# A second place for the residual sum, transposes that write every fourth column, and scales stored as 16 bytes per row

## The chip, the cores and the metric

The kernel runs on one core of a Trainium2 chip. The metric is the device time of one execution in microseconds (us). The kernel before took 1941.72 us, the median of 3 runs (1937.23 to 1942.7). The core has five engines with a queue each: TensorE (PE, with its weight loads listed apart as PEld), VectorE (DVE), ScalarE (ACT), GpSimd (POOL) and SyncE (SP, which here issues every DMA). An instruction that waits holds up all that stands behind it in its engine's queue.

## The reference

The input x is 8 images of 3136 positions by 256 channels. First stage: a real FFT over the positions, a complex 256x256 product with a bias, soft thresholding by 0.01, and the inverse FFT. Second stage, on its result x:

```python
X = np.fft.fft(x, axis=1); X = np.fft.fft(X, axis=2)
u = x + np.real(X)
un = (u - mean(u)) / sqrt(var(u) + 1e-6)      # per position, over 256 channels
out = u + relu(un @ w_ch1) @ w_ch2            # 256 -> 1024 -> 256
```

## The kernel before, in words

All transforms are matrix products. The 3136 positions are split as 64 x 49, so each image passes through a product over 64 (p1), one over 49 (p2_f2), the complex product with the weights (p2_w), the second FFT over channels (p2_mix), and back (p2_yt, p2_g2); these stages exchange their results through DRAM. Phase 3 then works on blocks of 128 positions. An even image has 24 blocks, in 6 groups of 4; an odd one has 25, in groups of 4, 4, 4, 4, 4, 2 and 3. That makes 52 groups for 8 images.

For each group phase 3 does this:

- p3_norm takes the last product of the inverse transform from PSUM and adds the term of the second FFT (line 714, tile ut, 128 positions x 256 channels, two blocks per tile, four buffers). It computes mean and variance, and from them rs, the reciprocal standard deviation of each position. The rs of a group are stored to a DRAM tile rd (line 737). The mean needs no correction later, as w1 and w2 are centred when they are loaded.
- p3_tr transposes ut on PE into PSUM (line 779, tile g_ut, one of the four "g" banks), so that channels lie on partitions, and splits it into a rounded half uth (ACT, line 781) and the remainder utl (DVE, line 156). Channels come as two halves k of 128. Before the change one step handles one pair of blocks with both halves k; a group of four blocks has two steps.
- p3_mlp1 multiplies by w1 (tile h) in eight slices f; each product is done as three products of halves. ReLU and the split into hh and hl follow (lines 798 and 799). After that POOL adds uth and utl into total (line 806), the residual, in four pieces of 256 columns. From then on uth and utl are free.
- p3_mlp2 multiplies by w2 into two PSUM banks (tile o) over the same eight slices. Between them it loads rb, the rs of the group spread over all partitions, from rd (line 824). At the end DVE multiplies o by rb (line 830; the second product is written into rb itself), adds it to total (line 833), and SP stores total to the output (line 834).

total has the tag "tot" with one buffer: the sum of a group can be written only when the stores of the group before have landed. The tile af, which holds the input of p2_f2 (line 446 loads it, two per quarter q of an image, lines 477 multiply), has three buffers of the same size, 4 KB per partition. cv_pair, a temporary of the weight split at the start, also lies in "tot".

Each stage is a generator that yields a due time; a heap runs them in order of these times, so that the instructions of many groups and images are interleaved in one program. Transposes are due from TR = -0.86 group times before their group, MLP 1 from 0 to 1, total at 1.0, and MLP 2 lags by MLAG/8 = 0.234. A planner of the framework then schedules the program by these priorities against its own model of time: an instruction moves forward to where the model finds its inputs and a free buffer. The order in each engine's queue is fixed at compile time; buffers are guarded by semaphores.

Of the kernel before, what the change touches and what calls it, by code (L numbers as in the profile page):

```python
# [10 lines left out]
F32 = mybir.dt.float32  # L11
F32R = mybir.dt.float32r
# [128 lines left out]
def spectral_block(ctx: ExitStack, tc: tile.TileContext, x, w_ri, b_ri, w1, w2,  # L141
# [30 lines left out]
    def split_double(name, h, l, parts, centred):  # L172

        def tmp(tag, bufs, dt=I32):
            return sb.tile([128, 512], dt, tag=tag, bufs=bufs, name=f"cv_{name}_{tag}")

        def v(t, sl):
            return t.rearrange("p (f e) -> p f e", f=h[sl].shape[1]) if len(h[sl].shape) == 3 else t  # L180

        both = []
        spare = centred and parts[0][0][2].start
        if spare:
            pair = sb.tile([128, 2, 512], F32R, tag="tot", bufs=1, name="cv_pair")
        for sl, raw in parts:
            hi, low = raw[:, 1::2], raw.bitcast(U16)[:, 1::4]
            tf = tmp("mt", 2, F32)
            sc.activation(tf, hi.bitcast(F32), AF.Abs, scale=65536.0)
            va.tensor_scalar(tf, tf, HI_MIN * 65536.0, HI_MAX * 65536.0, op0=ALU.max, op1=ALU.min)  # L190
            t = tf.bitcast(I32)
            va.tensor_scalar(t, t, 3, 0x7FFFFFFF, op0=ALU.logical_shift_left, op1=ALU.bitwise_and)
            w = tmp("ut", UTB)
            va.scalar_tensor_tensor(w, hi, -0x80000000, t, op0=ALU.bitwise_and, op1=ALU.bitwise_or)
            e = tmp("mt", 2)
            va.tensor_scalar(e, w, -0x800000, None, op0=ALU.bitwise_and)
            rf = pair[:, len(both)] if spare else tmp("ut", UTB, F32R)
            va.scalar_tensor_tensor(rf, low, 2.0 ** -36, e.bitcast(F32), op0=ALU.mult, op1=ALU.mult)
            both.append((sl, w.bitcast(F32), rf))
        if centred:  # L200
            mean = ps.tile([128, 512], F32, tag="h", bufs=2, name="mean")
            for i, (sl, wf, rf) in enumerate(both):
                te.matmul(mean, ones, wf, start=i == 0, stop=False)
                te.matmul(mean, share, rf, start=False, stop=i == 1)
            for sl, wf, rf in both:
                va.tensor_sub(wf, wf, mean)
        for sl, wf, rf in both:
            sc.copy(h[sl], v(wf, sl))
            va.tensor_sub(v(wf, sl), v(wf, sl), h[sl].bitcast(F32))
            va.tensor_add(l[sl], v(wf, sl), v(rf.bitcast(F32), sl))  # L210
# [230 lines left out]
    def rows_f2(b, q, s):  # L441

        u0 = 8 * q
        af = sb.tile([98, 4 * D], F32, tag="af", bufs=3, name="af")
        ad, u = a_dram[b](u0 + 4 * s)
        ld = nc.sync.dma_start(out=af.rearrange("p (u d) -> p u d", d=D), in_=ad.rearrange("n r c u d -> (n r c) u d")[:98, u:u + 4])
        tff = sb.tile([98, 4, 100], F32, tag="tff", bufs=3, name="tff")
        nc.sync.dma_start(out=tff, in_=c_tf[:, u0 + 4 * s:u0 + 4 * s + 4, :])
        if b == 0:
            af_ld[2 * q + s] = ld.ins  # L450
            done.add(("af", 2 * q + s))
        return af, tff
# [256 lines left out]
    def p3_norm(b):  # L709

        def finish(m, n, g, mt):

            ut = sb.tile([128, 2, D], F32, tag="ut", bufs=UTB, name="ut")
            va.tensor_add(ut[:, :n], g[:, :n * D].rearrange("p (n d) -> p n d", d=D), mt)
            gi, g0, z = [(i, g0, z) for i, (g0, z) in enumerate(GROUPS[b % 2]) if g0 <= m < g0 + z][0]
            if m == g0:
                scales[b, gi] = sb.tile([128, 4, 1], F32, tag="rs", bufs=4, name="rs")
            rall = scales[b, gi]
            rs = rall[:, m - g0:m - g0 + n]
            st = sb.tile([128, 2, 6], F32, tag="st", bufs=1, name="st")  # L720
            ag = sb.tile([128, 2, 2], F32, tag="ag", bufs=2, name="ag")
            for j in range(n):
                va.bn_stats(st[:, j], ut[:, j])
                va.bn_aggr(ag[:, j], st[:, j])
            vv = sb.tile([128, 2, 1], F32, tag="vv", bufs=1, name="vv")
            sc.activation(rs, ag[:, :n, 1:2], AF.Sqrt, bias=eps_t)
            gp.tensor_scalar(vv[:, :n], ag[:, :n, 1:2], 1.0, EPS, op0=ALU.mult, op1=ALU.add)
            va.reciprocal(rs, rs)

            gp.tensor_mul(vv[:, :n], vv[:, :n], rs)  # L730
            gp.tensor_mul(vv[:, :n], vv[:, :n], rs)
            gp.tensor_scalar(vv[:, :n], vv[:, :n], -0.5, 1.5, op0=ALU.mult, op1=ALU.add)
            gp.tensor_mul(rs, rs, vv[:, :n])
            uts[b, m] = ut
            if m + n == g0 + z:
                rd = scales[b, gi] = dr.tile([512], F32, tag="rd", bufs=4, name="rd")
                st_eng.dma_start(out=rd[:128 * z].rearrange("(j p) -> p j", j=z), in_=rall[:, :z].rearrange("p j o -> p (j o)"))
        for m, n in [(4 * i, 4) for i in range(6)] + [(NM - 1, 1)] * (b % 2):
            t0, T3 = clock3(b, m)
            yield t0 + T3 * (NRM - 0.5 * (n == 1))  # L740
            yield from after(("b", b), ("m", b))
            mt = sb.tile([128, 4, D], F32, tag="mt", bufs=2, name="mt")
            bfs = [sb.tile([128, 512], F32, tag="bf", bufs=4, name="bf") for _ in range(1 + (n > 1))]
            for r in range(2):
                if n == 1:
                    nc.sync.dma_start(out=bfs[0][64 * r:64 * r + 64, :D], in_=b_dram[b - 1 + r][m, 0].rearrange("c u d -> (c u) d"))
                else:
                    nc.sync.dma_start(out=bfs[r].rearrange("p (n d) -> p n d", d=D), in_=n2_rows(b_dram[b], m + 2 * r, 2))
            for r in (1, 0):
                bb, n2 = (b - 1 + r, m) if n == 1 else (b, NM * r + m)  # L750
                mpn, mmn = (d[0:NH].rearrange("(a n2) d -> a n2 d", n2=N2) for d in m_dram[bb])
                p = 64 * r
                nc.sync.dma_start(out=mt[p + 32:p + 64, :n][:, ::-1], in_=mmn[:, 49 - n2 - n:49 - n2])
                nc.sync.dma_start(out=mt[p:p + 32, :n], in_=mpn[:, n2:n2 + n])
            if n == 1:
                g = gtile("g_g1")
                te.matmul(g[:, :D], inv_f, bfs[0][:, :D], start=True, stop=True)
                finish(m, 1, g, mt[:, :1])
                continue
            banks = [gtile("g_g1") for _ in range(2)]  # L760
            quarters(banks, inv_f, [[bfs[r][64 * p:64 * p + 64] for r in range(2)] for p in range(2)], bfs[0][0:1, 0:2])
            for p, g in enumerate(banks):
                finish(m + 2 * p, 2, g, mt[:, 2 * p:2 * p + 2])

    def p3_tr(b):
        for gi, (g0, z) in enumerate(GROUPS[b % 2]):
            t0, T3 = clock3(b, g0)
            for i, n in parts_of[z]:
                yield t0 + T3 * (TR + i / 4)
                if i == 0:  # L770
                    uth = sb.tile([128, 2, 512], F32R, tag="uth", bufs=UTHB, name="uth")
                    utl = sb.tile([128, 2, 512], F32R, tag="utl", bufs=2, name="utl")
                    uthl[b, gi] = uth, utl
                ut = uts.pop((b, g0 + i))
                g = gtile("g_ut")
                gv = g.rearrange("p (k t) -> p k t", k=2)
                for j in range(n):
                    for k in range(2):
                        te.transpose(gv[:, k, j * 128:(j + 1) * 128], ut[:, j, k * 128:(k + 1) * 128], ident)  # L779
                tw = slice(i * 128, i * 128 + n * 128)  # L780
                sc.copy(uth[:, :, tw], gv[:, :, :n * 128])
                lo_v(utl[:, :, tw], gv[:, :, :n * 128], uth[:, :, tw])

    def p3_mlp1(b):
        for gi, (g0, z) in enumerate(GROUPS[b % 2]):
# [13 lines left out]
                va.scalar_tensor_tensor(hl[:, :w], h[:, :w], 0.0, hh[:, :w].bitcast(F32), op0=ALU.max, op1=ALU.subtract)  # L799
                hhl[b, gi, f] = hh, hl  # L800
            yield t0 + T3 * 1.0
            total = sb.tile([128, 2, 512], F32, tag="tot", bufs=1, name="total")
            for k in range(2):
                for c in range(0, w, D):
                    cols = slice(c, min(w, c + D))
# [3 lines left out]
    def p3_mlp2(b):  # L809
        for gi, (g0, z) in enumerate(GROUPS[b % 2]):  # L810
            t0, T3 = clock3(b, g0)
            w = z * 128
            for f in range(8):
# [5 lines left out]
                for k, o in enumerate(ops):  # L819
                    es = slice(k * 128, k * 128 + 128)  # L820
                    mm3(o, w2h[:, f, es], w2l[:, f, es], hh[:, :w], hl[:, :w], start=f == 0, stop=f == 7, first=1)
                if f == 1:
                    rb = sb.tile([128, 512], F32, tag="rb", bufs=1, name="rb")
                    nc.sync.dma_start(out=rb[:, :w], in_=scales.pop((b, gi))[:w].partition_broadcast(128))
            total = uthl.pop((b, gi))
# [105 lines left out]
```

## Time and profile before

| | |
|---|---|
| median of 3 runs | 1941.72 us |
| profiled execution, its own time | 1940.12 us |
| span of its instructions | 1938.3 us |
| mean granted TensorE clock | 0.973 |
| DMA queue of the program, share of 16 engines | 52.3% |

The profile is of a single execution. Its span runs from the first to the last instruction; 1.8 us lie around it. Busy shares are averages over the span. An idle time names what ended it, and a wait for several things is put down to the one that came last. In a timeline row the columns are start, duration, engine, line, operation, written tile <- read tiles, shape and count, and in brackets the idle time of the engine before it and who ended it.

### The profile page before, as it was taken

To read this page: it belongs to the slowest core of one execution; us is meant where nothing else is said; L and a number is where in the kernel's file an instruction comes from. 1 tells how busy PE (TensorE), PEld (TensorE's weight loads), DVE (VectorE), ACT (ScalarE), POOL (GpSimd) and SP (SyncE) were. 2 spreads that over 40 slices of the span, in tenths; PEclk is the share of its full clock that TensorE was granted. 3 is DMA by queue.
4 is the path that set the end of the run, shared out by engine and by line. 5 is a ranking of instruction groups with operands and counts; after the bars stand their busy time and mean duration, and the time that the engine had idled before them with its cause. 6 is when DMAs were issued, how large, how long until landed. Compare 5 with 4: busy or idle time off the path is not lost.

```text
span 1938.3 us, 29340 instructions
## 1 busy us (share of the span) xinstructions
PE 1841.4 (95%) x10044; PEld 1504.3 (78%) x10044; DVE 1192.2 (62%) x2603; ACT 807.5 (42%) x1864; POOL 560.4 (29%) x1028
## 2 busy tenths in 40 slices
PE   7886999899999999999999999999999999989998
PEld 4565787688787888877788788887878888867788
DVE  3664766566565766666666566656656656645543
ACT  2563544344444434444343444444444444322222
POOL 0003333222333422323323243332233433212121
PEclk8997999999999999999999999999999999999999
DMA  8763866455535756476444765546543543336211
GB/s 249 221 201 108 191 158 128 114 140 128 148 91 123 168 117 145 76 184 144 99 116 118 163 154 115 105 123 165 130 133 81 143 99 85 75 86 112 62 37 33
DMA packets 176365, 245.59 MB, mean 127 GB/s; under 512 B 42640, under 2 KB 123608, under 8 KB 175960
## 3 DMA queue, kind: packets, MB, share of 16 engines
q1 hardware_dynamic: 176216, 243.72, 52.3%
q8 instruction: 79, 1.29, 0.4%
q14 instruction: 70, 0.57, 0.1%
HBM read 140.79 MB, written 102.86 MB: 126 GB/s over the span
## 4 chain that ended last, share of the span: by engine, by line
PE 74%; DMA 12%; DVE 6%; POOL 3%; SPq 2%; issue 2%; ACT 2%; DVEq 0%; POOLq 0%; ACTq 0%
PE h L166 23%; PE o L166 23%; PE g_w L166 7%; PE g_f L477 4%; PE g_g L166 3%; DMA out_dram<-total 3%; PE g_g L377 2%; PE g_yt L665 2%; DMA mt<-md 2%; DMA bd<-bev 2%; PE g_ut L779 2%; PE g_f L377 2%; DMA xf<-in_x 2%; DMA md<-mq 1%; POOL total L806 1%
## 5 line engine op out<-in xcount | busy, mean ns | idle before, releaser
L799 DVE SCALAR_TENSOR_TENSOR hl<-h,hh 128x512 fp32r<-128x512 f32 (+2 forms) x416 | 273.1, 657 | 382.2 <-ACT hh L798 375.9
L798 ACT ACTIVATE hh<-h 128x512 fp32r<-128x512 f32 (+2 forms) x416 | 238.5, 574 | 417.3 <-PE h L166 396.5
L166 PE MATMUL o<-hl,w2h 128*128 128x512 f32 (+2 forms) x832 | 333.8, 401 | 9.9 <-DVE hl L799 7.6
L166 PE MATMUL h<-utl,w1h 128*128 128x512 f32 (+2 forms) x832 | 325.6, 391 | 2.8 <-DVE utl L156 2.8
L166 PE MATMUL h<-uth,w1l 128*128 128x512 f32 (+2 forms) x832 | 320.8, 386 | 0.0
L166 PE MATMUL h<-uth,w1h 128*128 128x512 f32 (+2 forms) x832 | 319.4, 384 | 0.0
L166 PE MATMUL o<-hh,w2l 128*128 128x512 f32 (+2 forms) x832 | 318.5, 383 | 0.0
L166 PE MATMUL o<-hh,w2h 128*128 128x512 f32 (+2 forms) x832 | 318.3, 383 | 0.0
L806 POOL TENSOR_TENSOR total<-uth,utl 128x256 f32<-128x256 f32 x200 | 146.4, 763 | 527.0 <-DMA out_dram<-total 404.2
L166 PEld LDWEIGHTS o<-hl,w2h 128*128 128x128 f32 x832 | 158.3, 190 | 47.1 <-DVE hl L799 13.5
L166 PEld LDWEIGHTS h<-utl,w1h 128*128 128x128 f32 x832 | 158.1, 190 | 35.8 <-issue 6.5
L166 PEld LDWEIGHTS h<-uth,w1l 128*128 128x128 f32 x832 | 158.2, 190 | 33.9 <-issue 4.1
L166 PEld LDWEIGHTS o<-hh,w2l 128*128 128x128 f32 x832 | 158.0, 190 | 29.7 <-issue 0.8
L166 PEld LDWEIGHTS h<-uth,w1h 128*128 128x128 f32 x832 | 158.3, 190 | 25.7
L166 PEld LDWEIGHTS o<-hh,w2h 128*128 128x128 f32 x832 | 158.6, 191 | 19.6
L477 PEld LDWEIGHTS g_f<-tff,af 98*128 98x128 f32 x1024 | 141.9, 200 | 32.5 <-DVE wdl L156 9.9
L477 PE MATMUL g_f<-tff,af 98*128 98x100 f32 x1024 | 150.3, 282 | 11.5 <-DMA af<-aq 9.1
L159 POOL TENSOR_TENSOR Xl<-xx,Xh 128x400 fp32r<-128x400 f32 x84 | 91.2, 1087 | 192.2 <-ACT Xh L494 188.9
L696 ACT COPY bev<-g_g 98x512 f32<-98x512 f32 x128 | 74.8, 585 | 113.9 <-PE g_g L166 59.2
L537 DVE SCALAR_TENSOR_TENSOR y<-g_w,bias,ks 128x400 f32<-128x400 f32 x128 | 80.5, 629 | 49.4 <-PE g_w L166 34.0
L540 POOL TENSOR_TENSOR Y<-y,m 128x400 f32<-128x400 f32 x56 | 62.5, 1117 | 166.5 <-DVE m L539 160.0
L665 PE MATMUL g_yt<-ident,Y 128*100 128x128 f32 x512 | 85.1, 281 | 24.5 <-POOL Y L544 7.8
(156 smaller groups left out, 3271.8 us busy)
## 6 DMA issues: line engine op xcount, KB each, us to landing
bd<-bev SPq DMA_DIRECT2D x128, 196.0 KB
bf<-bd SPq DMA_DIRECT2D x96, 256.0 KB
mt<-md SPq DMA_DIRECT2D x192, 128.0 KB
out_dram<-total SPq DMA_DIRECT2D x88, 256.0 KB
af<-ad SPq DMA_DIRECT2D x56, 392.0 KB
md<-mq SPq DMA_DIRECT2D x112, 192.0 KB
ad<-ev SPq DMA_DIRECT2D x84, 256.0 KB
xf<-in_x SPq DMA_DIRECT2D x39, 512.0 KB
```

The costliest lines, as they stand in the source:

```text
L159: gp.tensor_sub(out_, full, hi.bitcast(F32))
L166: te.matmul(o, l, r, start=start and i == 0, stop=stop and i == 2)
L377: return te.matmul(banks[i][64 * j:64 * j + 64], mat[rows, rows], movs[i][j], start=True, stop=True)
L477: te.matmul(gf[:, k, :, s], afs[s][:, ui * D + k * 128:ui * D + k * 128 + 128], tfs[s][:, ui].rearrange("p (c j) -> p c j", c=2), start=Tr ...
L537: va.scalar_tensor_tensor(y1, gw, bias[:, c, o:o + 1], ks, op0=ALU.add, op1=ALU.add)
L540: (va if b == 0 or o == 0 else gp).tensor_sub(y[:, o, :, c, :], y1, m)
L665: te.transpose(gt[:100, (v * 2 + o) * 128:(v * 2 + o + 1) * 128], y[:, o, place].rearrange("p c j -> p (c j)"), ident)
L696: sc.copy(bev, g[:98])
L779: te.transpose(gv[:, k, j * 128:(j + 1) * 128], ut[:, j, k * 128:(k + 1) * 128], ident)
L798: sc.activation(hh[:, :w], h[:, :w], AF.Relu)
L799: va.scalar_tensor_tensor(hl[:, :w], h[:, :w], 0.0, hh[:, :w].bitcast(F32), op0=ALU.max, op1=ALU.subtract)
L806: gp.tensor_add(total[:, k, cols], uth[:, k, cols].bitcast(F32), utl[:, k, cols].bitcast(F32))
```

## The change

1. "tot" gets two buffers and af two instead of three. For the first image, every third af tile (numbers 2 and 5 of its eight) takes a "tot" place.
2. p3_tr's steps go by half k instead of by pair of blocks. One step transposes one channel half of all z blocks of the group into one bank, block i into columns i, i + z, i + 2z, ..., so that position p of block i becomes column p*z + i. The second step is due 0.25 instead of 0.5 group times after the first. The copies then handle one half k of all z*128 columns.
3. In that order the rs of a group go out as z consecutive floats per partition (16 bytes for z = 4) where they were stored as single floats, block by block.
4. rb is loaded in slice f == 4 of MLP 2, where it was f == 1.
5. The host's unpacking of the output follows the new column order.

```diff
-            pair = sb.tile([128, 2, 512], F32R, tag="tot", bufs=1, name="cv_pair")
+            pair = sb.tile([128, 2, 512], F32R, tag="tot", bufs=2, name="cv_pair")
...
-        af = sb.tile([98, 4 * D], F32, tag="af", bufs=3, name="af")
+        tag = "tot" if b == 0 and (2 * q + s) % 3 == 2 else "af"
+        af = sb.tile([98, 4 * D], F32, tag=tag, bufs=2, name="af")
...
-                st_eng.dma_start(out=rd[:128 * z].rearrange("(j p) -> p j", j=z), in_=rall[:, :z].rearrange("p j o -> p (j o)"))
+                st_eng.dma_start(out=rd[:128 * z].rearrange("(p j) -> p j", j=z), in_=rall[:, :z].rearrange("p j o -> p (j o)"))
...
-            for i, n in parts_of[z]:
-                yield t0 + T3 * (TR + i / 4)
-                if i == 0:
+            w = z * 128
+            for k in range(2):
+                yield t0 + T3 * (TR + k / 4)
+                if k == 0:
                     uth = sb.tile([128, 2, 512], F32R, tag="uth", bufs=UTHB, name="uth")
                     utl = sb.tile([128, 2, 512], F32R, tag="utl", bufs=2, name="utl")
                     uthl[b, gi] = uth, utl
-                ut = uts.pop((b, g0 + i))
+                    blocks = [(uts[b, g0 + i], j) for i, n in parts_of[z] for j in range(n)]
                 g = gtile("g_ut")
-                gv = g.rearrange("p (k t) -> p k t", k=2)
-                for j in range(n):
-                    for k in range(2):
-                        te.transpose(gv[:, k, j * 128:(j + 1) * 128], ut[:, j, k * 128:(k + 1) * 128], ident)
-                tw = slice(i * 128, i * 128 + n * 128)
-                sc.copy(uth[:, :, tw], gv[:, :, :n * 128])
-                lo_v(utl[:, :, tw], gv[:, :, :n * 128], uth[:, :, tw])
+                gv = g[:, :w].rearrange("p (t j) -> p j t", j=z)
+                for i, (ut, j) in enumerate(blocks):
+                    te.transpose(gv[:, i], ut[:, j, k * 128:(k + 1) * 128], ident)
+                sc.copy(uth[:, k, :w], g[:, :w])
+                lo_v(utl[:, k, :w], g[:, :w], uth[:, k, :w])
...
-            total = sb.tile([128, 2, 512], F32, tag="tot", bufs=1, name="total")
+            total = sb.tile([128, 2, 512], F32, tag="tot", bufs=2, name="total")
...
-                if f == 1:
+                if f == 4:
                     rb = sb.tile([128, 512], F32, tag="rb", bufs=1, name="rb")
```

## Rows read from the trace of the kernel before

**Rows 1.** The page: busy time, share of the span and instructions of each engine; and the share of each engine in the chain of work that ended last.

```profile
PE 1841.4 (95%) x10044; PEld 1504.3 (78%) x10044; DVE 1192.2 (62%) x2603; ACT 807.5 (42%) x1864; POOL 560.4 (29%) x1028
...
PE 74%; DMA 12%; DVE 6%; POOL 3%; SPq 2%; issue 2%; ACT 2%; DVEq 0%; POOLq 0%; ACTq 0%
```

**Rows 2.** Two stretches of the span: length, busy time of PE, PEld, DVE, ACT and POOL, granted TensorE clock, DMA share, GB/s.

```profile
0.00:250.00 250.00, 206.51 (x1002) 147.41 (x1003) 144.77 (x324) 112.59 (x257) 39.20 (x72) 0.89 0.68 190
250.00:1750.00 1500.00, 1451.55 (x8152) 1206.43 (x8150) 958.74 (x2092) 647.09 (x1511) 487.84 (x863) 0.98 0.53 125
```

**Rows 3.** The longest entry of the waits of all engines: total us, times, longest us.

```profile
POOL total L806 <- DMA out_dram<-total: 404.2, 38, 20.6
```

**Rows 4.** The timeline of POOL and of DVE around one such wait.

```profile
949.54 2.80 POOL L806 TENSOR_TENSOR total<-uth,utl 128x256 f32<-128x256 f32 x4 [9.80 <-DMA out_dram<-total]
952.28 1.04 POOL L540 TENSOR_TENSOR Y<-y,m 128x400 f32<-128x400 f32 x1
...
953.36 2.78 DVE L575 SCALAR_TENSOR_TENSOR eo<-Y,mask 128x200 f32<-128x200 f32 x2 [6.93 <-POOL Y L540]
```

**Rows 5.** The timeline of PE: the matmuls in front of which PE stood idle, and which the chain of waits puts behind a wait as in rows 4.

```profile
335.31 0.51 PE L166 MATMUL g_g<-yl,tih 100*98 100x256 f32 x1 [4.63 <-DVE Xl L156]
...
378.06 0.88 PE L665 MATMUL g_yt<-ident,Y 128*100 128x128 f32 x3 [7.45 <-POOL Y L544]
...
492.06 0.53 PE L665 MATMUL g_yt<-ident,Y 128*100 128x128 f32 x3 [2.41 <-POOL Y L540]
495.48 0.69 PE L477 MATMUL g_f<-tff,af 98*128 98x100 f32 x4 [1.04 <-DVE ev L423]
...
843.62 0.50 PE L166 MATMUL o<-hl,w2h 128*128 128x512 f32 x1 [1.26 <-DVE hl L799]
...
953.38 0.53 PE L665 MATMUL g_yt<-ident,Y 128*100 128x128 f32 x3 [2.46 <-POOL Y L540]
...
1304.37 0.50 PE L166 MATMUL o<-hl,w2h 128*128 128x512 f32 x1 [1.17 <-DVE hl L799]
...
1411.00 0.53 PE L665 MATMUL g_yt<-ident,Y 128*100 128x128 f32 x3 [2.10 <-POOL Y L540]
...
1564.01 0.58 PE L166 MATMUL o<-hl,w2h 128*128 128x256 f32 x1 [4.23 <-DVE hl L799]
...
1683.43 0.50 PE L166 MATMUL o<-hl,w2h 128*128 128x512 f32 x1 [0.53 <-DVE hl L799]
```

**Rows 6.** Stretches of the span that begin with such an idle time; columns as in rows 2, the granted clock is the third number from the end.

```profile
330.00:342.00 12.00, 7.37 (x32) 6.25 (x32) 5.52 (x12) 5.29 (x12) 5.46 (x8) 0.72 0.55 185
376.00:392.00 16.00, 13.94 (x77) 12.10 (x78) 6.62 (x13) 9.81 (x22) 6.87 (x10) 0.84 0.58 166
...
950.00:962.00 12.00, 9.46 (x42) 7.08 (x42) 7.24 (x10) 6.10 (x14) 7.54 (x9) 0.86 0.39 121
...
1409.00:1421.00 12.00, 9.92 (x47) 7.97 (x48) 7.68 (x12) 7.34 (x18) 7.27 (x9) 0.86 0.36 105
...
1562.00:1576.00 14.00, 11.99 (x79) 11.79 (x83) 11.26 (x25) 8.71 (x24) 8.67 (x8) 0.76 0.18 50
```

**Rows 7.** The transposes of phase 3: one step in the timeline of PE; then, for all that touches the tile g_ut, duration in ns (least, median, most), first and last start and forms.

```profile
940.17 0.60 PE L779 MATMUL g_ut<-ident,ut 128*128 128x128 f32 x4
...
L779 PE MATMUL g_ut<-ident,ut x392: 270/272/474, 165.7 to 1862.8; 128*128 128x128 f32 x196
...
L156 DVE TENSOR_TENSOR utl<-g_ut,uth x100: 411/681/694, 167.6 to 1903.6; 128x512 fp32r<-128x512 f32 x96, 128x256 fp32r<-128x256 f32 x4
```

**Rows 8.** The timeline of PE and SP around one change of quarter: the last products of one quarter's af, a load of the next, and the first products of that. Ahead of them, one load from the chain of work (start of the issue, us until it landed).

```profile
193.83 8.04 DMA af<-ad
...
848.47 0.59 PE L477 MATMUL g_f<-tff,af 98*128 98x100 f32 x4
...
855.50 0.35 SPq L446 DMA_DIRECT2D af<-ad  x1
...
894.67 1.14 PE L477 MATMUL g_f<-tff,af 98*128 98x100 f32 x8
```

**Rows 9.** The load of rb and the first use of it in the timeline; and two entries of the waits of SP's queue (total us, times, longest us).

```profile
941.81 1.66 SPq L824 DMA_DIRECT2D rb<-rd  x1
...
979.80 0.68 DVE L830 TENSOR_TENSOR t<-o,rb 128x512 f32<-128x512 f32 x1
...
SPq L698 <- ACT bev L696: 126.6, 35, 11.5
...
SPq L748 <- PE g_g L377: 85.0, 15, 16.2
```

**Rows 10.** Two more sums in the timeline of POOL, one while DVE stood still, one while it worked.

```profile
329.95 2.79 POOL L806 TENSOR_TENSOR total<-uth,utl 128x256 f32<-128x256 f32 x4 [6.77 <-DMA out_dram<-total]
...
1338.20 3.46 POOL L806 TENSOR_TENSOR total<-uth,utl 128x256 f32<-128x256 f32 x4 [15.47 <-DMA out_dram<-total]
```

**Rows 11.** Two stores of total in the chain of work (start of the issue, us until it landed), and the second ACT copy into uth of a group in ACT's timeline.

```profile
318.25 11.52 DMA out_dram<-total
...
941.40 7.98 DMA out_dram<-total
...
963.16 0.58 ACT L781 CAST uth<-g_ut 128x512 fp32r<-128x512 f32 x1
```

**Rows 12.** The page: all DMA packets.

```profile
DMA packets 176365, 245.59 MB, mean 127 GB/s; under 512 B 42640, under 2 KB 123608, under 8 KB 175960
```

More of the change, by code (lines that the diff above doesn't have):

```diff
@@ L918 @@
             at = s * (NM - 1) + g0
-            y[:, :, at:at + z] = raw[:, :, at * D:(at + z) * D].reshape(nb // 2, 128, 2, z, 128).transpose(0, 4, 3, 2, 1)
+            y[:, :, at:at + z] = raw[:, :, at * D:(at + z) * D].reshape(nb // 2, 128, 2, 128, z).transpose(0, 3, 4, 2, 1)
     y = y.reshape(nb // 2, 2, 2, 32, N2, D)
```

## Prediction

> **What bounds the kernel now.** I began with the busy shares and the shares of the chain that ended last. PE is busy for 95% of the span and holds 74% of the chain [rows 1]: the kernel is bound by PE, and a change that adds no PE work can only give back time in which PE stands idle or runs at its lower clock. Then I read the stretches. In the first 250 us, the start-up, PE is idle for 250 - 206.5 = 43.5 us; in the 1500 us behind it for 1500 - 1451.6 = 48.5 us [rows 2]. The change touches the start-up little, so the 48.5 us are the stock.
>
> The waits of all engines come next. The longest is POOL's, for the landing of the output stores before it may write total: 404.2 us in 38 of the 52 groups [rows 3]. Idle time of POOL alone costs nothing, so the question is what stands behind it in POOL's queue. One group shows it [rows 4]: total begins at 949.54 after 9.80 us of waiting; behind it the thresholded Y is written at 952.28; DVE had waited 6.93 us for that Y; and PE's transposes of Y begin at 953.38 after 2.46 us of idle time [rows 5]. So a store's landing stops POOL, POOL stops DVE, and DVE and POOL stop PE. I followed the chain of waits through every idle time of PE above 0.5 us behind the start-up; the ones that it leads back to a wait of total are in rows 5. They sum to 4.63 + 7.45 + 2.41 + 1.04 + 1.26 + 2.46 + 1.17 + 2.10 + 4.23 + 0.53 = 27.3 us, over half of the stock.
>
> PE loses more than that. In five stretches the granted clock is 0.72 to 0.86 after PE had stood idle [rows 6], and it has only two levels, 1.2 and 2.4 GHz. The time at the lower one is thus twice the missing share: 2 x (0.28 x 12 + 0.16 x 16 + 0.14 x 12 + 0.14 x 12 + 0.24 x 14) = 25.3 us, and half of it, 12.6 us, is lost. Together 27.3 + 12.6 = 40 us hang on the wait of total.
>
> **The change part by part.** *The second place for total.* The sum of a group then needs the stores of the group before the last, a group time earlier. A group lasts 35.5 us: 13 groups lie between the same transposes at 492.06 and 953.38 [rows 5]. A store needs 8 to 11.5 us to land [rows 11]. So the landing leaves the chain where total is ready at the old place in the queue. What is late next is total's inputs. The planner puts total as early as it finds a place, so total will move up to the last copies of uth and utl, and part 2 moves these up as well. The second copy now starts at 963.16, when the stores issued at 941.40 landed at 949.4 [rows 11]; due 0.25 x 35.5 = 8.9 us earlier it starts near 954, and utl follows by some 2 us. The slack is about 954 + 2 - 949 = 7 us there, and 3.5 us less behind a landing of 11.5 us. So some totals still wait, a few us where it was 10. I take a quarter of the 40 us back for this, 10 us; the ends are 0 (the slack holds everywhere) and 40 (POOL stops as long as before, with another name).
>
> The sum moves from a time in which DVE stands still to one in which it works. Four pieces of total took 2.79 us with DVE idle and up to 3.46 us with DVE working [rows 10], 0.67 us more. At the ten places of rows 5 that is at most 6.7 us of POOL, beside PE. I take 0, as POOL is busy for only 29% of the span [rows 1]. The Trainium skill, page "SBUF — State Buffer", section "Who interferes with whom", has a rule that speaks against the change here: a DVE instruction with two SBUF inputs competes with a GpSimd instruction that reads SBUF for the read interface that the two share. The trace agrees in direction with those 0.67 us, and by the rule at its worst the gain would be 6.7 us smaller.
>
> *The steps by channel half.* The number of transposes stays 392, as do the steps for groups of 4 and 3 blocks. A step of four now occupies PE from 940.17 for 0.60 us, with 0.272 us for one [rows 7]: (0.60 - 0.27)/3 = 0.11 us from one to the next. Four groups of two blocks get a second copy and subtraction: 4 x 0.41 us on DVE by the smallest form [rows 7], and as much on ACT, hidden beside PE; 3 us over both if not. The first step now needs both tiles ut; they are finished one behind the other on DVE and MLP 1 needs both halves anyway, so I take 0. What the trace doesn't show is a transpose that writes every fourth column. The lower end is 0, the upper the slowest transpose in the trace, 0.474 - 0.272 = 0.20 us more each [rows 7], 392 x 0.20 = 79 us. I take 0, because each column is still one float per partition and 0.11 us per transpose is the pace now; the upper end is a rival.
>
> *Two places for af.* Two loads per quarter now both wait for the products of the quarter before. That costs SP's queue nothing new where the loads are issued behind those products already: at 855.50 a load went out after the last products at 848.47 and 39 us before the first use at 894.67 [rows 8]. A load took 8.0 us on the chain [rows 8], so the cost is 0; where a load stands too early in SP's queue it stops the stores behind it, between 0 and some 10 us in all. The first image keeps three places, two of them under another tag.
>
> *The scales.* A store of 512 floats becomes one of 128 rows of 16 bytes. The packets under 512 bytes are 42640 of 176365 [rows 12], of which 44 x 512 + 4 x 256 + 4 x 384 = 25,088 are these; they become 6,656. Nobody on the chain waits for rd, so I take 0 for it, with the small gain that the stores of total queued beside it land sooner.
>
> *rb later.* It was issued right behind the store, at 941.81, and used at 979.80 [rows 9], 38 us ahead. Three eighths of a group time later is 13.3 us less: 25 us remain. Cost 0, unless the planner places it later still.
>
> **Sum.** 40 - 10 = 30 us by the terms. Time given back to a PE-bound queue isn't all kept, as the remaining 48.5 - 27.3 = 21 us of idle time hang on DMA landings and PSUM copies that now come due earlier, and the planner will order everything anew. I take off 6 us, about a quarter of those 21 us: 24 us are left. The profiled execution took 1940.1 us (span 1938.3 and 1.8 around it), so 1916.1; it lay 1.6 us below the median of the runs shown, so about 1917 in a run.
>
> **Rivals.**
> *More than that.* All 40 us go and the newly ordered queue has fewer idle times: 1941.7 - 45 = about 1896. For it: the slack of 7 us above. Against: a gap closed at one place often opens at the next late input.
> *The wait changes its name.* total stands as early in POOL's queue as a free place allows and waits for utl instead, with Y behind it. Then POOL stops DVE as before and the time is about 1939. For it: in 38 of 52 groups total stands right behind a landing [rows 3], the earliest place that it can have now. Against: utl comes from DVE within us, a store lands after 8 to 11.5.
> *rb comes late (slower).* SP's queue stops for up to 16.2 us for PE and 11.5 us for ACT [rows 9]. Were rb placed by its new priority, about 13 us before its use, a stop of over 5 us (13 less a landing of 8, as a store's in rows 11) makes DVE's multiplication wait, and the two banks of o with it. If that strikes 15 groups by 5 us, 75 us, less the gain of 24: about 1993; by 3 us, 1963. It decides from a lead under 13 us.
> *Strided transposes are slow (slower).* If one takes a further 0.11 us, twice its pace, 392 of them cost 43 us and the time is 1917 + 43 = 1960; against the gain it decides from 0.06 us on. For it: no operation of the trace writes so. Against: they are 392 of 10044 matmuls, and their pace is not that of the writes alone.
>
> **How the numbers follow.** The forecast has 0.45 (own range 1908 to 1930), more than that 0.16, the wait by another name 0.14, slow transposes 0.09, late rb 0.08, and a worse order by the planner of any other kind 0.08 (1945 to 1955). A measurement of this kernel can tell about 0.3%, 6 us. Faster takes the first two and a quarter of the third, 0.65; same gets 0.10 and slower the rest, 0.25. The range leaves out the better half of the second case and most of the slow ends: 1888 to 1958.
>
> **What would show it.** Right: POOL's wait of total for out_dram falls from 404 us to under 100 us, the idle times of rows 5 are gone, the mean clock is above 0.973, total stands shortly behind utl, and a step of four transposes still takes about 0.60 us. Wrong: total waits as long for another tile, a transpose of 0.4 us, DVE waiting for rb, or new idle times of PE above 1 us at other places that sum to more than 20 us.

## The result and the profile after

The changed kernel takes 1868.78 us (median of 4 runs, 1865.7 to 1872.6) where the kernel before took 1939.47 us in the same set (4 runs, 1935.45 to 1942.7): a ratio of 0.9637 with a 95% interval of 0.961 to 0.9665, 70.7 us less. The prediction was 1917 us in a range of 1888 to 1958: the direction was right, the size far off.

The profiled execution took 1868.51 us, with a span of 1866.6 us and a mean granted clock of 0.987. The page of the changed kernel, busy shares and chain, answers to [rows 1]:

```profile
PE 1818.2 (97%) x10044; PEld 1491.0 (80%) x10044; DVE 1190.1 (64%) x2607; ACT 807.9 (43%) x1868; POOL 558.1 (30%) x1028
...
PE 88%; DVE 5%; DMA 3%; SPq 1%; ACT 1%; issue 1%; POOL 0%; DVEq 0%; ACTq 0%; POOLq 0%
```

DMA has all but left the chain: from 12% to 3%. Stretches of the span of the changed kernel, columns as in [rows 2]:

```profile
0.00:250.00 250.00, 210.61 (x1038) 151.26 (x1039) 148.54 (x328) 113.02 (x260) 42.10 (x75) 0.91 0.66 196
250.00:1680.00 1430.00, 1425.97 (x8121) 1190.24 (x8120) 954.11 (x2097) 647.49 (x1513) 485.83 (x865) 1.00 0.45 130
```

PE was idle for 48.5 us in the long middle; now it is idle for 1430 - 1426 = 4 us. The start-up lost 4 us of its 43.5 us of idle time. The third part is the clock: PE's busy time fell by 1841.4 - 1818.2 = 23.2 us for the same 10044 matmuls, with the granted clock of the middle at 1.00 where it was 0.98. Together 44.4 + 4.1 + 23.2 = 71.7 us, the whole difference of the spans. So nearly the full stock of idle time came back, and nearly twice the clock loss (23.2 us against 12.6 us) that the prediction had put down to the wait of total.

The timeline of PE in the changed kernel, all idle times above 0.5 us behind the start-up; it answers to the ten of [rows 5]:

```profile
322.55 0.50 PE L166 MATMUL o<-hl,w2h 128*128 128x512 f32 x1 [2.21 <-DVE hl L799]
...
363.36 0.51 PE L166 MATMUL o<-hl,w2h 128*128 128x512 f32 x1 [0.63 <-DVE hl L799]
...
1676.71 1.25 PE L780 MATMUL g_ut<-ident,ut 128*128 128x128 f32 x8 [0.64 <-DVE ut L715]
```

And the waits of all engines in the changed kernel (total us, times, longest us), the entries on POOL's sum and on what DVE waits for behind it; the first answers to [rows 3]:

```profile
POOL total L806 <- DMA out_dram<-total: 297.9, 34, 19.6
...
POOL total L806 <- DVE utl L156: 74.6, 28, 8.9
...
DVE eo L576 <- POOL Y L541: 15.9, 15, 1.8
```

This doesn't fit the forecast. POOL still waits for the landing of the stores, 298 us in 34 groups, with a second place for the sum; the prediction asked for under 100 us. Yet PE no longer stands still. The longest wait of DVE for Y behind POOL's sum fell from 6.9 us [rows 4] to 1.8 us. The last view that changed much is the page's count of DMA packets and the program's DMA queue; the first line answers to [rows 12], and the queue's share was 52.3% with the same 243.72 MB:

```profile
DMA packets 157932, 245.58 MB, mean 132 GB/s; under 512 B 24208, under 2 KB 105176, under 8 KB 157528
...
q1 hardware_dynamic: 157784, 243.72, 44.6%
```

The same bytes take 7.7 points less of 16 DMA engines. So there were two theories beside the one that the planner's new order did it (C): the stores of the scales in single floats held up all DMA (A), or the second place for the sum freed the time as predicted (B).

### The profile page after: what moved, and what is told of

Same layout as the page of the kernel before. It is cut to its first block, busy times and chain, and to the rows that moved or that the text cites. A ratio compares the mean times of both kernels' runs of the same rounds, so it can differ in the third digit from the quotient of the medians.

```text
span 1866.6 us, 29317 instructions
## 1 busy us (share of the span) xinstructions
PE 1818.2 (97%) x10044; PEld 1491.0 (80%) x10044; DVE 1190.1 (64%) x2607; ACT 807.9 (43%) x1868; POOL 558.1 (30%) x1028
## 3 DMA queue, kind: packets, MB, share of 16 engines
q1 hardware_dynamic: 157784, 243.72, 44.6%
## 4 chain that ended last, share of the span: by engine, by line
PE 88%; DVE 5%; DMA 3%; SPq 1%; ACT 1%; issue 1%; POOL 0%; DVEq 0%; ACTq 0%; POOLq 0%
PE o L166 28%; PE h L166 28%; PE g_w L166 9%; PE g_f L478 5%; PE g_g L166 4%; PE g_yt L666 3%; PE g_g L377 2%; PE g_ut L780 2%; PE g_f L377 2%; PE g_mix L598 2%; DMA raw_w<-in_w 1%; PE g_w L524 1%; PE g_f L341 1%; PE g_mix L600 1%; DVE eo L576 1%
## 5 line engine op out<-in xcount | busy, mean ns | idle before, releaser
L697 ACT COPY bev<-g_g 98x512 f32<-98x512 f32 x128 | 74.6, 583 | 61.1 <-PE g_g L166 49.7
L159 POOL TENSOR_TENSOR Xsl<-xs,Xsh 128x200 fp32r<-128x200 f32 x112 | 71.5, 639 | 76.0 <-ACT Xsh L504 75.4
```

The costliest lines, as they stand in the source:

```text
L159: gp.tensor_sub(out_, full, hi.bitcast(F32))
L697: sc.copy(bev, g[:98])
```

## The experiments

Each set of runs stood beside the kernel before on the same chip, three chips in all; the kernel before took 1924 to 1926 us in each (medians of 6 to 13 runs), less than the 1939 us of the first set. Times are medians, ratios have their 95% interval.

### 1. The form of the stores alone, put in and taken out

In the kernel before (e1_before_rd16), and reversed in the changed kernel (e2_after_rd4):

```diff
-                st_eng.dma_start(out=rd[:128 * z].rearrange("(j p) -> p j", j=z), in_=rall[:, :z].rearrange("p j o -> p (j o)"))
+                st_eng.dma_start(out=rd[:128 * z].rearrange("(p j) -> p j", j=z), in_=rall[:, :z].rearrange("p j o -> p (j o)"))
```

> The kernel before with one edit: the scales of a group are stored as 16 bytes per partition instead of single floats. It leaves the transposes as they were, so the scales reach other positions than they belong to; everything else is computed as before, and the order of the instructions is the same on PE, DVE, ACT and POOL. Theory A (the scattered four-byte stores hold up the DMA engines, and the landings of everything else with them): most of the 71 us come from here, 1880 to 1905 us, the DMA queue's share falls from 52% to about 45% and POOL's wait of total for the landing of the output stores falls by a third or more. Theory B (the second place for the sum is what freed the time, as predicted): within 6 us of the kernel before, 1934 to 1946 us, with the DMA share a little lower. Theory C (the planner's new order did it): the same as B.

> The changed kernel with one edit: the scales go out as single floats, block by block, as before the change; so they reach other positions than they belong to, everything else is computed as in the changed kernel, and the order of the instructions is the same on PE, DVE, ACT and POOL. Theory A: it loses 30 us or more, 1900 to 1930 us, with the DMA share back at 52%. Theory B and C: within 6 us of the changed kernel, 1863 to 1875 us.

Measured: 1871.25 us put in, ratio 0.9732 (0.9705 to 0.9759), 55.0 us less than before. Taken out of the changed kernel: 1895.11 us, ratio 0.9852 (0.9827 to 0.9878). Theory A holds in both directions, though not in size; B and C had asked for no change. Put in, the new stores gave more than A had asked for (1880 to 1905 us). POOL's wait for the landing fell from 404 to 314 us, 22% where A asked for a third or more. Taken out, they cost 29 us (26 us against the first set), a little less than the 30 us and the 1900 us that A asked for, with the queue's share back at 52.0%. So the same edit is worth 55 us in one kernel and 29 us in the other; part 5 comes back to this. The engines that compute run the same instructions in the same order in each pair, so what differs is how long DMA takes. In the kernel with this single edit, the queue's share on the page, and its long middle, columns as in [rows 2]:

```profile
q1 hardware_dynamic: 157784, 243.72, 44.8%
```

```profile
250.00:1682.00 1432.00, 1427.90 (x8135) 1191.62 (x8134) 962.23 (x2094) 649.35 (x1512) 487.74 (x862) 1.00 0.45 130
```

PE is idle for 4 us there, as in the changed kernel. As the order is that of the kernel before, single events can be compared. (The only trace of the kernel before is of the first set, so a part of the difference can be the chip's; the kernels of part 4 ran on one chip.) The store issued at 941.40 in the kernel before took 7.98 us to land [rows 11], and POOL waited 9.80 us for it [rows 4]. Its counterpart, in the chain of work and in POOL's timeline of this kernel:

```profile
906.79 3.96 DMA out_dram<-total
...
910.91 2.84 POOL L806 TENSOR_TENSOR total<-uth,utl 128x256 f32<-128x256 f32 x4 [5.78 <-DMA out_dram<-total]
```

The landing takes half as long, POOL's wait is 4.0 us shorter, and the idle time of PE of 2.46 us [rows 5] is gone. With one place for the sum as before, POOL waits 314 us in 37 groups: the wait remains, and here at most its last 4 us had been on the path.

### 2. The second place for the sum, alone and taken out

```diff
-            total = sb.tile([128, 2, 512], F32, tag="tot", bufs=1, name="total")
+            total = sb.tile([128, 2, 512], F32, tag="tot", bufs=2, name="total")
...
-        af = sb.tile([98, 4 * D], F32, tag="af", bufs=3, name="af")
+        tag = "tot" if b == 0 and (2 * q + s) % 3 == 2 else "af"
+        af = sb.tile([98, 4 * D], F32, tag=tag, bufs=2, name="af")
```

> The kernel before with the second place for the sum alone (af with two places, the third one for the first image under the other tag). Theory A: little by itself, 1920 to 1940 us, as the landings stay slow. Theory B: 1895 to 1917 us, the idle times of PE behind a wait of total gone. Theory C: anything, as the planner orders all engines anew.

> The changed kernel with one place for the sum and three for af, as before the change; the rest of the change stays. Theory A: it keeps most of the gain, 1875 to 1900 us. Theory B: it loses 30 to 45 us, 1898 to 1915 us, with POOL's wait of total for the stores back in front of idle times of PE.

Measured: alone 1917.3 us (10 runs), ratio 0.996 (0.9944 to 0.9976), 9 us less. Taken out of the changed kernel: 1872.43 us, ratio 0.9736 (0.9711 to 0.976). Alone it stands at the slow edge of what theory B asked for, 3 us below what A did; but taking the place out costs 6 us, at the edge of what can be told, where B asked for 30 to 45, and there B falls. (A had asked for 1875 to 1900 us, and 1872 us is a little faster.) The waits of the kernel with the second place alone show why:

```profile
POOL total L807 <- DMA out_dram<-total: 413.1, 39, 19.8
POOL total L807 <- DVE utl L156: 99.7, 28, 15.7
```

The planner moves the sum forward by as much as the second place allows. It then stands behind the landing of the store that frees this place, 39 times instead of 38, and that landing is as slow as before. POOL's timeline shows the sum of one group, now in two parts of two pieces; the second part waits for utl:

```profile
897.31 1.45 POOL L807 TENSOR_TENSOR total<-uth,utl 128x256 f32<-128x256 f32 x2 [4.75 <-DMA out_dram<-total]
...
906.70 1.44 POOL L807 TENSOR_TENSOR total<-uth,utl 128x256 f32<-128x256 f32 x2 [7.38 <-DVE utl L156]
```

In PE's timeline of that kernel there are still stalls of the kind of [rows 5], two of them near the places at 843.62 and 953.38, where it was 1.26 and 2.46 us:

```profile
826.83 0.50 PE L166 MATMUL o<-hl,w2h 128*128 128x512 f32 x1 [3.47 <-DVE hl L800]
...
935.66 0.53 PE L666 MATMUL g_yt<-ident,Y 128*100 128x128 f32 x3 [1.68 <-POOL Y L541]
```

### 3. The changed kernel again, and its parts

The changed kernel on this chip (e5_after_again, no edit); the kernel before with the edits of 1 and 2 together (e6_before_tot2_rd16); and two small edits of the changed kernel, each by itself (e7_after_f1, e8_after_k2):

```diff
-                if f == 4:
+                if f == 1:
```

```diff
-                yield t0 + T3 * (TR + k / 4)
+                yield t0 + T3 * (TR + k / 2)
```

> The changed kernel as it is, beside the kernel before on the chip of this set, so that the runs of this and the last set can be set against it by their ratios. Its ratio was 0.9637 (0.961 to 0.9665); the small stores alone gave 0.9732 and the change without the second place for the sum 0.9736. Theory A with a part for the second place: again 0.961 to 0.967, so that the second place is worth near 1% once the stores are cheap. Theory A alone: 0.970 to 0.975, the first ratio being partly the chip's.

> The kernel before with the second place for the sum (and two places for af) and the scales stored as 16 bytes per partition, the transposes and the load of rb left as they were, so that the scales reach other positions than they belong to. If these two edits make the whole change: the ratio of the changed kernel within 0.003. If the transposes by channel half, or rb in a later slice, have a share of their own: 0.970 or more, near the 0.9732 of the small stores alone.

> The changed kernel with rb loaded in slice f == 1 again. SP's order of instructions is the same as in the changed kernel, that of PE, DVE, ACT and POOL differs in places. If the later slice matters only through these: within 0.3% of the changed kernel either way. If a load earlier than needed was in the way: 5 us or more slower.

> The changed kernel with the second channel half due half a group time after the first instead of a quarter. If the earlier second half gives total its inputs in time, it loses 3 us or more, with more of POOL's wait named utl; if it pushes total up against the landing of the stores, as the prediction feared, it is the same or up to 5 us faster, with less of POOL's wait named out_dram.

Measured: the changed kernel 1866.37 us, ratio 0.9692 (0.9668 to 0.9715), between the two forms of theory A. On this chip the change is worth 59.6 us, 92% of which the form of the stores gives alone. The two edits together: 1868.01 us, 0.9693 (0.967 to 0.9716), the whole change within what can be told. rb in slice 1: 1868.9 us, 0.9697 (0.9675 to 0.972), no difference. The second channel half at half a group time: 1875.16 us, 0.9736 (0.9716 to 0.9757), 8.8 us slower. The waits of that kernel have the sign that was asked for, the wait named utl nearly doubled against 74.6 us:

```profile
POOL total L806 <- DMA out_dram<-total: 284.4, 33, 19.9
POOL total L806 <- DVE utl L156: 140.0, 31, 16.0
```

But this wait isn't what costs the 8.8 us. Two stretches of that kernel, columns as in [rows 2], beside those of the changed kernel above:

```profile
0.00:250.00 250.00, 204.57 (x995) 146.25 (x996) 147.56 (x323) 111.20 (x256) 41.25 (x75) 0.89 0.65 193
250.00:1680.00 1430.00, 1425.46 (x8119) 1191.68 (x8119) 959.62 (x2090) 648.71 (x1512) 485.50 (x858) 1.00 0.44 129
```

In the first 250 us it does 995 matmuls where the changed kernel did 1038; in the long middle it does 8119 against 8121 in the same time. The time is lost in the start-up, and there the earlier second half has a use. In the middle neither wait of POOL decides: e6 too has 142.8 us of waiting for utl and is as fast as the changed kernel.

### 4. What makes the small stores dear

Behind each store of the scales in the changed kernel stands a second one, into a DRAM tile rx that nothing reads. Four forms, with the same order on PE, DVE, ACT and POOL (the last stores one float per partition, 128 in all):

```diff
+                rx = dr.tile([512], F32, tag="rx", bufs=4, name="rx")
+                st_eng.dma_start(out=rx[:128 * z].rearrange("(p j) -> p j", j=z), in_=...)     # e9
+                st_eng.dma_start(out=rx[:128 * z].rearrange("(j p) -> p j", j=z), in_=...)     # e10
+                st_eng.dma_start(out=rx[:128 * z, 0].rearrange("(j p) -> p j", j=z), in_=...)  # e11, rx is [512, 128]
+                st_eng.dma_start(out=rx[:128].rearrange("(p j) -> p j", j=1), in_=...)         # e12
```

> The changed kernel with a second store of each group's scales behind the first, into a DRAM tile that nothing reads, in 128 rows of 16 bytes as the first. The base of this set: all four have the same order of instructions on PE, DVE, ACT and POOL, and one further store in each of 52 groups. Expected within 0.5% of the changed kernel, 1864 to 1876 us, and the DMA queue's share within 1% of its 44.6%.

> As the base of this set, but the further store goes out as single floats block by block, as the scales did before the change: up to 512 floats, side by side in DRAM, neighbouring floats from neighbouring partitions. Theory A: the share of the DMA queue rises by 6 to 8 points as it did in the kernel before, and the time by 20 to 45 us over the base. If the price lay elsewhere in the old store than in the DMA engines (in what waits for rd, for instance): no more than 5 us over the base, as nothing waits for this store.

> As the single floats of this set, in the same number and order, but each into a place of its own, 512 bytes from the next. If the price is one per small store: the same as the single floats side by side. If it comes from many DMA engines storing pieces of one stretch of memory at once: near the base, within 6 us, with the share of the DMA queue within 2 points of the base.

> As the base of this set, but the further store has one float per partition, 128 floats side by side: a quarter of the small stores of the single-float variant, and as many as the base. If the price is one per small store, whatever its size: the base, within 5 us. If it goes with floats side by side: about a quarter of the rise of the DMA share of the 512 floats, 1.5 to 2 points over the base, and a third of its time or less.

Measured, with the ratio to the kernel before and the queue's share from each page:

```
e9   128 rows of 16 bytes               1868.78 us  0.97   (0.9676 to 0.9723)  44.9%
e10  512 single floats, side by side    1901.97 us  0.9876 (0.9849 to 0.9902)  52.6%
e11  512 single floats, 512 bytes apart 1867.61 us  0.9699 (0.9677 to 0.972)   45.6%
e12  128 single floats, side by side    1874.97 us  0.9738 (0.9714 to 0.9762)  48.7%
```

The queue's line on the page of e10 and on that of e11:

```profile
q1 hardware_dynamic: 183704, 243.83, 52.6%
```

```profile
q1 hardware_dynamic: 183704, 243.83, 45.6%
```

The packets and bytes of the two are equal to the last digit, and so is the order of the work; only the addresses in DRAM differ. Side by side the floats cost 33 us over the base e9, apart they cost nothing. Beside e9, the queue of e10 takes 52.6% x 1895.8 - 44.9% x 1868.1 = 158 us more of each of 16 engines; spread over its 44 x 512 + 4 x 256 + 4 x 384 = 25,088 floats that is 0.10 us per float. In e11, by the same sum with a span of 1864.9 us, it is 12 us, 0.01 us per float.

The floats' own packets don't take this time. (A packet is the piece of a transfer that one DMA engine moves at a time; the traces keep the duration of each.) The packets of four bytes take 9 ns in the median in e10 and in e11, and 27 and 24 us of each engine in all. What differs is how often another packet is held up: in e10, 284 packets took more than 2.5 us, none of them a single float, and nearly all of these end 5 to 12 us after the issue of such a store; in e11 there are none. The kernel before has 346, the changed kernel 2. Nothing waits for the added stores, so the time is lost by the transfers beside them.

My estimate for e12, a quarter of the rise in share, was too low: the share rises by half as much with a quarter of the floats, 0.17 us for each by the same sum; its time, 6 us over the base, is within the third that was expected. It has as many small stores as e9, of 4 bytes where those have 16, so their number is not the cause either.

### 5. What the transposes by half are worth with the old stores

With the old form of the stores, the changed kernel (e2) had still been 31 us faster than the kernel before, while the second place alone gave 9. Two kernels leave both the old stores and one place for the sum: the transposes by half with rb in slice 4 (e13_halves_f4_rd4) and with rb in slice 1 (e14_halves_rd4, the kernel before with p3_tr and the host's unpacking replaced and nothing else).

```diff
-            for i, n in parts_of[z]:
-                yield t0 + T3 * (TR + i / 4)
+            for k in range(2):
+                yield t0 + T3 * (TR + k / 4)
...
+                    te.transpose(gv[:, i], ut[:, j, k * 128:(k + 1) * 128], ident)
```

> The changed kernel with the old form of the stores of the scales (so that they reach other positions than they belong to), one place for the sum and three for af: what is left of the change is the transposes by channel half and rb in slice f == 4. If these bring the remaining 22 us whenever the old stores slow the landings: 1898 to 1908 us. If they help only together with the second place: 1920 to 1930 us, that of the kernel before.

> As the other run of this set, but rb is loaded in slice f == 1 as before the change: the transposes by channel half alone, with the old form of the stores (the scales reach other positions than they belong to). If the transposes by half are what helps: within 6 us of the other run. If the later load of rb is: 10 us or more slower than it.

Measured: 1902.79 us, 0.988 (0.9861 to 0.9898), and 1902.0 us, 0.9882 (0.9867 to 0.9898). The transposes by half alone are worth 24 us as long as the stores are slow, and rb's slice nothing. With quick stores they are worth nothing that can be told: 1872.43 us for the change without the second place against 1871.25 us for the stores alone. Three edits answer the same idle times of PE, alone 55, 24 and 9 us, and 60 us together. Whether the 24 us come from the earlier second half or from another order of the planner's was not tried; e8, which has quick stores and lost its time in the start-up, doesn't tell.

## Why the prediction was wrong

**What bounds the kernel: right, but it stopped one step short.** PE is the bound, its idle times and its clock were the stock, and the path from a store's landing over POOL's sum, Y and DVE to PE is real: with the landing shortened by 4.0 us and nothing else moved, the stall behind it is gone. The stock was also larger than the share that was counted. All 48.5 us in the middle but 4 came back, not only the 27.3 us led back to the sum, and 23.2 us of clock, not 12.6 us. In e1, where only the times of DMA differ, PE is idle for the same 4 us: the other stalls hung on DMA as well.

**The step that failed is the term for the scales.** "Nobody on the chain waits for rd, so I take 0 for it": that term measured 55 us alone. The question put to the trace was who waits for this store. The question that counted is what the store takes from the transfers beside it. The "small gain that the stores of total queued beside it land sooner" was most of the matter: 55 us alone, and still 29 us where the rest of the change stands. The trace of before had a sign of it: two stretches of the kernel before, the first ahead of any store of scales, and the same two of the changed kernel (DMA share and GB/s are the last numbers).

```profile
0.00:100.00 100.00, 78.78 (x306) 49.26 (x306) 54.13 (x122) 39.28 (x82) 0.41 (x6) 0.88 0.79 239
600.00:700.00 100.00, 96.55 (x599) 82.55 (x592) 64.68 (x151) 46.70 (x114) 34.15 (x58) 0.97 0.71 160
```

```profile
0.00:100.00 100.00, 80.26 (x314) 50.20 (x314) 54.53 (x123) 39.09 (x82) 0.41 (x6) 0.88 0.79 242
600.00:700.00 100.00, 99.78 (x622) 85.83 (x621) 70.21 (x158) 46.31 (x113) 35.46 (x62) 1.00 0.52 147
```

At the start 79% of the engines' time moved 239 GB/s, 3.0 GB/s per point; in the middle 71% moved 160 GB/s, 2.3 per point. After the change the start is the same and the middle has 2.8 per point. The transfers of the start and of the middle differ, so this was a hint and no proof: engines that are busy for few bytes were to be seen, though not why.

**The second place for the sum: credited with 30 of 40 us, measured 9 alone and 6 or 3 with quick stores** (e4 against e5, at the edge of noise; e1 against e6, within it). The first half of the step held: the sum moved forward. The rival "the wait changes its name" had the mechanism, but with a narrower turn: POOL waits for the landing as long as before, of another group's store, and for utl besides (99.7 us in e3). "The landing leaves the chain" assumed that the sum stays at its old place in POOL's queue, which a planner that fills every free place doesn't grant. The 0 us taken for a sum beside a working DVE held: a piece of it took 763 ns on average before and after.

**The steps by channel half: 0 was taken, and 24 us with slow stores, 0 with quick ones, was measured.** The rival of slow strided transposes is out. The timeline of one step in the changed kernel, and the duration of all (ns, least, median, most), beside [rows 7]:

```profile
867.67 0.60 PE L780 MATMUL g_ut<-ident,ut 128*128 128x128 f32 x4
...
L780 PE MATMUL g_ut<-ident,ut x392: 270/272/447, 162.1 to 1791.3; 128*128 128x128 f32 x196
```

A transpose that writes every fourth column takes the 272 ns of one that writes neighbouring columns, and four take 0.60 us as before.

**rb later, af with two places: 0, as forecast.** e7 shows the first; for the second, e6 has two places for af and isn't slower than e1. The rival of a late rb didn't occur.

**The sum of 30 us, less 6 us for the planner's new order: near the truth by luck.** The change without the new stores (e2) gave 31 us. But the second place, which was to bring the 30 us, is worth 9 us alone, and the steps by half, taken at 0, bring 24. No run shows the 6 us by themselves. The last step of the sum, 1916.1 + 1.6, is 1917.7 us and not about 1917, which changes nothing.

## What to carry to other kernels

Ask of a small transfer not only who waits for it but what it does to the transfers beside it; if it can be spared or stored in rows, try that first. A DMA share that is high for the GB/s beside it is a sign to follow. When several waits end in DMA landings, a faster landing shortens them all, while one more buffer shortens one of them, and a planner may spend the buffer on moving the same wait elsewhere.

## What the runs showed of the hardware that was not expected

Single floats that neighbouring partitions store side by side in DRAM hold up other transfers: 0.10 us of engine time per float with 512 of them in a store and 0.17 us with 128 (e10, e12), and 0.01 us when the 512 lie 512 bytes apart, at the same count and size (e11). The packets of the floats stay at 9 ns in the median; packets of other transfers take over 2.5 us, 284 times in e10, 181 in e12 and never in e11. Rows of 16 bytes side by side cost nothing that shows (e9, also without such a packet). The Trainium skill, page "DMA: Bandwidth & Descriptors", section "Specifications", says that a transfer below 512 bytes is done by reading, changing and writing back. No run here shows the reading back, and the size alone doesn't make the price here: the floats of e11 are as small as those of e10. How near two stores must lie, and where between 4 and 16 bytes the price begins, was not tried.

The kernel before took 1939 us in the first set and 1924 to 1926 us on the three chips of the others, the changed kernel 1869 us and, on one of the three, 1866 us. That the stores side by side cost more on one chip than on another would fit, but it wasn't shown.
